# Cluster-routed attention with an ELU feed-forward on one core: query masks move to VectorE, the products lag one block more, and the weight conversion is spread more thinly

## The chip, the core and the metric

The kernel runs on one core of a Trainium2 chip. The core has a matrix engine (TensorE, PE in the profile, with its weight loads as PEld), three engines for elementwise work (VectorE is DVE, ScalarE is ACT, GpSimd is POOL) and a queue for transfers (SP). Each engine works through its own instructions in order and waits for the others through semaphores. The metric is the device time of one execution in microseconds (us).

## The reference, cut to what matters

```python
# q, k, v: (4 batches, 8 heads, 768 tokens, 64) float32; centroids: (8 heads, 16, 64)
q_assign = argmax(q_n @ c_n.T)            # nearest of 16 centroids for each query ...
k_assign = argmax(k_n @ c_n.T)            # ... and each key, by normalised rows
mask   = q_assign[:, :, :, None] == k_assign[:, :, None, :]
scores = where(mask, q @ k.T / 8, -1e9)   # a query sees the keys of its own cluster
attn   = softmax(scores)
x      = (attn @ v)  ->  (3072 tokens, 512)
h      = x @ w_in                         # w_in: (512, 2048)
g      = where(h > 0, h, exp(min(h, 0)) - 1)
out    = g @ w_out                        # w_out: (2048, 512)
```

The inputs q, k, v and the centroids are float32. The two weight matrices are float64 (float32 numbers divided by a numpy square root), so the kernel gets 64-bit words and makes float32 of them on the chip.

## The kernel before

**Blocks.** A batch has three thirds of 256 queries and four pairs of heads, so there are 48 blocks (batch, third, pair). The main loop runs over n: it finishes block n-1 (`values`), prepares the mask of block n+1 (`masks`), makes the scores of block n (`scores`), and then takes one group of the feed-forward, LAG blocks behind. A third of a batch has four groups: two calls of `hidden`, two more with a closing `finish`, four products of `outer`, three products of `outer`. (The seven products stand for eight by sums of blocks, a Strassen-like scheme, which is why the weights are summed once.)

In the code below the line numbers that the profile uses are put beside the lines as comments; `...` marks cuts.

```python
def masks(n):                                   # hot: one-hot cluster of each token, bf16
    b, third, pr = blocks[n]
    qm[n] = route.tile([P, QS], BF16, name="qm", tag="qm", bufs=2)
    for e in range(2):
        rows = slice(64 * e, 64 * e + 64)
        m = big[rows, pr % 2 : pr % 2 + 1]
        nc.gpsimd.tensor_scalar(                                        # L374
            qm[n][rows], hot[b, 0][rows, side(pr, e), ts(third, QS)],
            m, m, op0=Alu.mult, op1=Alu.subtract)

LAG = 6

def scores(n):
    ...
    for u in range(NT // 2):                    # three times a block
        s = banks()                             # one of three PSUM slots
        ...                                     # q.k on PE, L401
        ...                                     # + hot_k . qm on PE (the mask), L410
        nc.scalar.activation(p, s, Act.Exp, scale=SCALE)                # L418
        if n < LAG + 2:
            weigh(1)

def sums(n):                                    # three adds on VectorE   L424, L425, L426
    ...
def values(n):
    d = banks()[:, 0]
    summed = osum.pop(n, None)
    ...                # p.v into o_bank, 24 matmul instructions          # L447
    ...                # row sums of p: 24 instructions, or 4 where sums(n) has run   # L436
    nc.scalar.copy(x, o_bank[:, :QS])                                   # L461
    nc.scalar.activation(r, d[:, :QS], Act.Copy, accum_out=...)         # L463
    nc.vector.reciprocal(r, r)                                          # L464
    nc.gpsimd.tensor_tensor(x, x, r, op=Alu.mult)                       # L465

def hidden(b, third, n):
    h = banks()
    ...                                         # 32 matmul instructions, L486
    nc.scalar.activation(t, hf, Act.Exp)                                # L496
    nc.gpsimd.tensor_scalar(t, t, 1.0, 0.0, op0=Alu.min, op1=Alu.max)   # L497
    finish()                                    # the elu of the hidden before this
    lag.append(lambda: elu(n, t, hf))
def elu(n, t, hf):
    nc.vector.scalar_tensor_tensor(t, t, -1.0, hf, op0=Alu.add, op1=Alu.max)   # L503
    ...                                         # and a sum of blocks, L505 or L507
```

**Conversion of the weights.** `weigh(k)` takes the next k of 34 steps. The 32 pieces (16 of w_in, 16 of w_out, 128 x 512 each) pass through three consecutive steps each:

```python
for n in range(len(pieces) + 2):
    if n < len(pieces):
        e = exps[n] = loads.tile([P, WC], U32, name="ex", tag="ex", bufs=3)
        nc.vector.tensor_scalar(pieces[n][0], high, 0xFFFFF, ...)       # L244
        nc.vector.tensor_scalar(e, high, 0x7FF00000, ...)               # L247
    if 0 <= n - 1 < len(pieces):
        nc.scalar.activation(ex, ex, Act.Relu, scale=8.0, bias=off)     # L250
        nc.gpsimd.tensor_scalar(to, to, 2.0**-20, 1.0, ...)             # L251
    if n > 1:
        nc.vector.scalar_tensor_tensor(ex, w[:, :, 1], ..., ex, ...)    # L257
        nc.vector.scalar_tensor_tensor(to, w[:, :, 0], ..., to, ...)    # L260
        nc.gpsimd.tensor_tensor(to, to, ex, op=Alu.mult)                # L263
        ...
    yield
```

When all are done, `sum_weights` makes sums of blocks of w_out, in two halves: per half two GpSimd operations (L295, L296) and two VectorE ones (L297, L298).

**The main loop.**

```python
for n in range(len(blocks) + LAG):
    b, at = n // NB, n % NB                     # NB = 12 blocks a batch
    if 0 < n <= len(blocks): values(n - 1)
    ...
    if n + 1 < len(blocks) and at + 1 < NB: masks(n + 1)
    if n < len(blocks): scores(n)
    if 0 < n <= len(blocks): check(n - 1)       # L471
    if n < len(blocks):
        if n >= LAG + 2: sums(n)
        if ahead and at in turns: ...           # transposes of q and k of the next batch, L310
    beside = []
    if ahead and at + 1 == NB:                  # last block of a batch: clusters of the next
        beside = [None, similar(q), assign(q), similar(k), assign(k), masks(n + 1)]
    main = groups[n - LAG] if n >= LAG else []
    if n == LAG + 2:
        weigh(100)
        for half in range(2): sum_weights(half)
    for m, step in enumerate(main):
        step()
        ...                                     # beside is dealt out evenly behind the steps
        if n < LAG + 2: weigh(2)
```

`similar` is a matmul (L331) and a VectorE transpose (L338); `assign` is a chain on VectorE (L348, L350, L360, L363) that ends in `hot`.

Of the kernel before, what the change touches and what calls it, by code (L numbers as in the profile page):

```python
# [60 lines left out]
def main_path(ctx, tc, c, q, k, v, centroids, moe_w_in, moe_w_out, out):  # L61
    nc = tc.nc
# [31 lines left out]
    def banks():  # L94
        return short.tile([P, 2, 512], F32, name="banks", tag="banks")
# [13 lines left out]
    def load(name, i):  # L109
        b, pr = pairs[i]  # L110
        src = {"q": q, "k": k, "v": v}[name]
        if (name, i) in staged:
            t = first[:, ts(staged[name, i], 2 * NT * D)]
        elif name == "v":
            t = loads.tile([P, 2 * NT * D], F32, name="v_raw", tag="v", bufs=2)
        else:
            t = loads.tile([P, 2 * NT * D], F32, name=f"{name}_raw", tag="raw", bufs=4)
        if name == "v" or name == "q" and b == 0:
            t = t.rearrange("p (h t d) -> p h t d", h=2, t=NT)
            nc.sync.dma_start(  # L120
                t.rearrange("p h t d -> p h (t d)"),
                src[b, 2 * pr : 2 * pr + 2].rearrange("h (p t) d -> p h (t d)", t=NT),
            )
        elif b == 0:
            t = t.rearrange("p (t h d) -> p t h d", t=NT, h=2)
            for e in range(2):
                nc.sync.dma_start(
                    t[:, :, e], src[b, 2 * pr + e].rearrange("(p t) d -> p t d", t=NT)
                )
        else:  # L130

            for e in range(2):
                for g in range(2):
                    at = 64 * e + 32 * g
                    nc.sync.dma_start(
                        t[at : at + 32].rearrange("p (t a d) -> p t a d", t=NT, d=32),
                        src[b, 2 * pr + e, :, 32 * g : 32 * g + 32].rearrange(
                            "(a p t) d -> p t a d", a=4, t=NT
                        ),
                    )  # L140
        raw[name, i] = t
# [133 lines left out]
    def weigh(n):  # L275
        for _ in range(n):
            next(rest, None)
# [87 lines left out]
    def side(pr, e):  # L365
        return int(pr // 2 != e)

    def masks(n):
        b, third, pr = blocks[n]
        qm[n] = route.tile([P, QS], BF16, name="qm", tag="qm", bufs=2)  # L370
        for e in range(2):
            rows = slice(64 * e, 64 * e + 64)
            m = big[rows, pr % 2 : pr % 2 + 1]
            nc.gpsimd.tensor_scalar(  # L374
                qm[n][rows],
                hot[b, 0][rows, side(pr, e), ts(third, QS)],
                m,
                m,
                op0=Alu.mult,
                op1=Alu.subtract,  # L380
            )


    LAG = 6

# [3 lines left out]
    def scores(n):  # L391
        b, third, pr = blocks[n]
        i = b * NPR + pr
        cols = ts(third, QS)
        for u in range(NT // 2):
            s = banks()
            for m in range(2):
                kt = 2 * u + m
                for e in range(2):
                    rows = slice(64 * e, 64 * e + 64)  # L400
                    nc.tensor.matmul(  # L401
                        s[:, e, ts(m, QS)],
                        lhsT=T[i, 1][rows, ts(kt, P)],
                        rhs=T[i, 0][rows, cols],
                        start=True,
                        stop=False,
                    )
                for e in range(2):
                    rows = slice(64 * e, 64 * e + 64)
                    nc.tensor.matmul(  # L410
                        s[:, e, ts(m, QS)],
                        lhsT=hot[b, 1][rows, side(pr, e), ts(kt, P)],
                        rhs=qm[n][rows],
                        start=False,
                        stop=True,
                    )
            p = pu[n, u] = probs.tile([P, 2, 2 * QS], F32, name="p", tag="p")
            nc.scalar.activation(p, s, Act.Exp, scale=SCALE)  # L418
            if n < LAG + 2:
                weigh(1)  # L420

    def sums(n):
# [5 lines left out]
# [6 lines that stand above are left out]
        def row_sums(p, m, kt, last):  # L434
            for e in range(2):
                nc.tensor.matmul(  # L436
                    d[64 * e : 64 * e + 64, :QS],
                    lhsT=ones,
                    rhs=p[:, e, ts(m, QS)],
                    start=(kt == 0),  # L440
                    stop=(kt == last),
                )

        for kt in range(NT):
            p, m = pu[n, kt // 2], kt % 2
            for e in range(2):
                nc.tensor.matmul(  # L447
                    o_bank[64 * e : 64 * e + 64, :QS],
                    lhsT=raw["v", n][:, e, kt],
                    rhs=p[:, e, ts(m, QS)],  # L450
                    start=(kt == 0),
                    stop=(kt == NT - 1),
                )
            if summed is None:
                row_sums(p, m, kt, NT - 1)
        if summed is not None:
            row_sums(summed, 0, 0, 0)
        if pr == 0:
            xT[b, third] = xtp.tile([P, KC, QS], F32, name="xT", tag="xT")
        x = xT[b, third][:, pr]  # L460
        nc.scalar.copy(x, o_bank[:, :QS])  # L461
        r = work.tile([P, QS], F32, name="r", tag="r", bufs=1)
        nc.scalar.activation(r, d[:, :QS], Act.Copy, accum_out=d_sum[:, n : n + 1])  # L463
        nc.vector.reciprocal(r, r)  # L464
        nc.gpsimd.tensor_tensor(x, x, r, op=Alu.mult)  # L465
        rs[n] = r

    def check(n):

        r = rs.pop(n)  # L470
        nc.scalar.activation(r, r, Act.Copy, accum_out=r_sum[:, n : n + 1])  # L471
# [131 lines left out]
    def load_v(n):  # L603
        b, third, pr = blocks[n]
        if n not in seen:
            seen.add(n)
            load("v", b * NPR + pr)
            raw["v", n] = raw.pop(("v", b * NPR + pr))
# [3 lines left out]
    for j in range(2):  # L612
        for pr in range(NPR):
            turn(pr, j)
        for half in range(2):
            similar(0, j, half)
            assign(0, j, half)
        if j == 0:
            masks(0)

    for n in range(len(blocks) + LAG):
        b, at = n // NB, n % NB
        ahead = b + 1 < B
        if n <= len(blocks) and n > 0:
            values(n - 1)
        if ahead:
            for pr in {5: [0], 6: [1], 9: [2], 10: [3]}.get(at, []):
                load("q", (b + 1) * NPR + pr)
                load("k", (b + 1) * NPR + pr)
        if n + 1 < len(blocks):  # L630
            load_v(n + 1)
        if n + 1 < len(blocks) and at + 1 < NB:
            masks(n + 1)
        if n < len(blocks):
            scores(n)
        if 0 < n <= len(blocks):
            check(n - 1)
        if n < len(blocks):
            if n >= LAG + 2:
                sums(n)  # L640
            if ahead and at in turns:
                for j in range(2):
                    turn((b + 1) * NPR + turns[at], j)
        beside = []
        if ahead and at + 1 == NB:
            beside.append(None)
            for j in range(2):
                beside.append(lambda b=b, j=j: [similar(b + 1, j, half) for half in range(2)])
                beside.append(lambda b=b, j=j: [assign(b + 1, j, half) for half in range(2)])
            beside.append(lambda n=n: masks(n + 1))  # L650
# [3 lines that stand above are left out]
            for half in range(2):  # L654
                sum_weights(half)
        done = 0
        for m, step in enumerate(main):
            step()
            upto = len(beside) * (m + 1) // len(main)
            for other in beside[done:upto]:  # L660
                if other:
                    other()
            done = upto
            if n < LAG + 2:
                weigh(2)
        for other in beside[done:]:
            if other:
                other()
# [268 lines left out]
```

## Time and profile before

| | us |
|---|---|
| device time, median of three runs | 1076.47 (1075.84 to 1077.30) |
| span of the profiled execution | 1076.1 |
| VectorE busy in it | 523.3 (49%) |
| ScalarE busy | 292.8 (27%) |
| GpSimd busy | 332.2 (31%) |
| GpSimd in the query masks (L374), 96 instructions | 145.6, mean 1516 ns |

A row of the groups gives the line, the engine, the operation, what it writes and reads, how often, its busy time with the mean of one, and then the idle time of that engine just before it with what ended it. A busy PE is not PE at its peak, since the ends of matmuls are modelled. So the table of stretches (busy time of each engine between two moments) and the chain of waits say more of PE than its busy share.

### The profile page before, as it was taken

To read this page: it belongs to the slowest core of one execution; us is meant where nothing else is said; L and a number is where in the kernel's file an instruction comes from. 1 tells how busy PE (TensorE), PEld (TensorE's weight loads), DVE (VectorE), ACT (ScalarE), POOL (GpSimd) and SP (SyncE) were. 2 spreads that over 40 slices of the span, in tenths; PEclk is the share of its full clock that TensorE was granted. 3 is DMA by queue.
4 is the path that set the end of the run, shared out by engine and by line. 5 is a ranking of instruction groups with operands and counts; after the bars stand their busy time and mean duration, and the time that the engine had idled before them with its cause. 6 is when DMAs were issued, how large, how long until landed. Compare 5 with 4: busy or idle time off the path is not lost.

```text
span 1076.1 us, 14909 instructions
## 1 busy us (share of the span) xinstructions
PE 1014.5 (94%) x6363; PEld 785.1 (73%) x6363; DVE 523.3 (49%) x641; ACT 292.8 (27%) x499; POOL 332.2 (31%) x291
## 2 busy tenths in 40 slices
PE   7868785899999999999999999999999999999997
PEld 5545564676877877876887877876787877877885
DVE  5666677548425425538524425538534424424131
ACT  3544322132223123122223223122313223222010
POOL 2677778222322223122322222222322222221010
PEclk9999896999999999999999999999999999999999
DMA  9626511030001121230001120221000001000000
GB/s 286 243 69 162 137 55 30 15 79 16 16 35 42 34 64 30 44 69 27 15 35 38 37 64 30 44 65 30 16 35 30 16 35 31 16 35 1 20 1 23
DMA packets 103961, 55.60 MB, mean 52 GB/s; under 512 B 83408, under 2 KB 96720, under 8 KB 103888
## 3 DMA queue, kind: packets, MB, share of 16 engines
q1 hardware_dynamic: 103888, 54.57, 18.5%
q8 instruction: 52, 0.85, 0.3%
q14 instruction: 21, 0.17, 0.1%
HBM read 48.27 MB, written 6.29 MB: 51 GB/s over the span
## 4 chain that ended last, share of the span: by engine, by line
PE 78%; DVE 10%; POOL 8%; issue 3%; ACT 0%; DMA 0%; POOLq 0%; DVEq 0%
PE banks L486 27%; PE f_bank L516 15%; PE o_bank L516 11%; PE banks L401 10%; PE o_bank L447 10%; POOL qm L374 3%; PE banks L410 3%; DVE ex L257 2%; PE banks L436 2%; DVE r L464 1%; POOL w_in L263 1%; POOL w_out L263 1%; DVE ex L247 1%; DVE w_out L260 1%; DVE gT L503 1%
## 5 line engine op out<-in xcount | busy, mean ns | idle before, releaser
L486 PE MATMUL banks<-xT,w_in 128*128 128x256 f32 x1536 | 338.9, 381 | 0.3
L486 PEld LDWEIGHTS banks<-xT,w_in 128*128 128x128 f32 x1536 | 290.2, 190 | 48.2 <-issue 4.1
L401 PE MATMUL banks<-qT,kT 64*128 64x256 f32 x1152 | 175.8, 403 | 22.7 <-DVE gT L503 15.4
L418 ACT ACTIVATE p<-banks 128x1024 f32<-128x1024 f32 x144 | 147.2, 1022 | 52.3 <-PE banks L410 48.1
L447 PE MATMUL o_bank<-p,v_raw 128*64 128x256 f32 x1152 | 142.4, 384 | 11.1 <-ACT p L418 11.1
L374 POOL TENSOR_SCALAR qm<-hot,big 64x256 bf16<-64x256 bf16 x96 | 145.6, 1516 | 21.5 <-DVE hot L360 16.7
L464 DVE RECIPROCAL r<-r 128x256 f32<-128x256 f32 x48 | 84.0, 1750 | 133.7 <-ACT r L463 133.6
L401 PEld LDWEIGHTS banks<-qT,kT 64*128 64x128 f32 x1152 | 91.3, 194 | 75.0 <-DVE gT L503 16.7
L497 POOL TENSOR_SCALAR gT<-gT 128x1024 f32<-128x1024 f32 x48 | 51.2, 1067 | 277.3 <-ACT gT L496 277.3
L503 DVE SCALAR_TENSOR_TENSOR gT<-gT,banks 128x1024 f32<-128x1024 f32 x48 | 58.4, 1216 | 141.9 <-POOL gT L497 141.1
L447 PEld LDWEIGHTS o_bank<-p,v_raw 128*64 128x64 f32 x1152 | 78.1, 136 | 64.5 <-issue 16.1
L496 ACT ACTIVATE gT<-banks 128x1024 f32<-128x1024 f32 x48 | 49.1, 1022 | 275.5 <-PE banks L486 275.5
L465 POOL TENSOR_TENSOR xT<-xT,r 128x256 f32<-128x256 f32 x48 | 38.5, 801 | 274.6 <-DVE r L464 274.6
L516 PE MATMUL o_bank<-w_out,gT 128*128 128x256 f32 x384 | 91.4, 392 | 8.8 <-POOL w_out L296 8.7
L516 PEld LDWEIGHTS o_bank<-w_out,gT 128*128 128x128 f32 x384 | 73.7, 195 | 23.6 <-POOL w_out L296 9.9
L410 PE MATMUL banks<-qm,hot 64*128 64x256 bf16 x576 | 83.6, 276 | 4.5 <-DVE hot L360 4.4
L516 PE MATMUL f_bank<-w_out,gT 128*128 128x256 f32 x384 | 86.8, 379 | 0.0
L516 PEld LDWEIGHTS f_bank<-w_out,gT 128*128 128x128 f32 x384 | 73.0, 190 | 9.9
L461 ACT COPY xT<-o_bank 128x256 f32<-128x256 f32 x48 | 17.7, 369 | 219.6 <-PE o_bank L447 219.6
L424 DVE TENSOR_TENSOR psum<-p 128x1024 f32<-128x1024 f32 x40 | 51.7, 1293 | 37.8 <-ACT p L418 37.8
L425 DVE TENSOR_TENSOR psum<-psum,p 128x1024 f32<-128x1024 f32 x40 | 55.5, 1387 | 4.4 <-ACT p L418 0.6
L516 PE MATMUL f_bank<-w_sum,g_sum 128*128 128x256 f32 x192 | 44.6, 386 | 1.2 <-DVE part L563 1.2
(108 smaller groups left out, 832.7 us busy)
## 6 DMA issues: line engine op xcount, KB each, us to landing
v_raw<-in_v_dram SPq DMA_DIRECT2D x48, 384.0 KB, 3.2
w_sum<-in_moe_w_out_dram SPq DMA_DIRECT2D x12, 512.0 KB, 3.6
out_dram<-o_sb SPq DMA_DIRECT2D x24, 256.0 KB, 2.0
q_raw<-in_q_dram SPq DMA_DIRECT2D x48, 96.0 KB, 3.2
k_raw<-in_k_dram SPq DMA_DIRECT2D x48, 96.0 KB, 3.3
w_sum<-in_moe_w_in_dram SPq DMA_DIRECT2D x8, 512.0 KB, 7.5
w_out<-in_moe_w_in_dram SPq DMA_DIRECT2D x8, 512.0 KB, 10.4
w_out<-in_moe_w_out_dram SPq DMA_DIRECT2D x4, 512.0 KB, 4.1
```

Of the source, the lines that this page charges most:

```text
L374: nc.gpsimd.tensor_scalar(qm[n][rows], hot[b, 0][rows, side(pr, e), ts(third, QS)], m, m, op0=Alu.mult, op1=Alu.subtract,)
L401: nc.tensor.matmul(s[:, e, ts(m, QS)], lhsT=T[i, 1][rows, ts(kt, P)], rhs=T[i, 0][rows, cols], start=True, stop=False,)
L410: nc.tensor.matmul(s[:, e, ts(m, QS)], lhsT=hot[b, 1][rows, side(pr, e), ts(kt, P)], rhs=qm[n][rows], start=False, stop=True,)
L418: nc.scalar.activation(p, s, Act.Exp, scale=SCALE)
L424: nc.vector.tensor_tensor(to, pu[n, 0], pu[n, 1], op=Alu.add)
L425: nc.vector.tensor_tensor(to, to, pu[n, 2], op=Alu.add)
L447: nc.tensor.matmul(o_bank[64 * e : 64 * e + 64, :QS], lhsT=raw["v", n][:, e, kt], rhs=p[:, e, ts(m, QS)], start=(kt == 0), stop=(kt == NT ...
L464: nc.vector.reciprocal(r, r)
L486: nc.tensor.matmul(hf[:, f], lhsT=w_in[:, ch, ts(4 * n + f, P)], rhs=xT[b, third][:, ch], start=(ch == 0 and f % 2 == 0), stop=(ch == KC - 1),
L497: nc.gpsimd.tensor_scalar(t, t, 1.0, 0.0, op0=Alu.min, op1=Alu.max)
L503: nc.vector.scalar_tensor_tensor(t, t, -1.0, hf, op0=Alu.add, op1=Alu.max)
L516: nc.tensor.matmul(to[:, :QS], lhsT=left[:, f], rhs=right[:, f], start=(f == 0), stop=(f == FC // 2 - 1),)
```

## The change

The query masks go from GpSimd to VectorE. The feed-forward runs seven blocks behind attention instead of six. The conversion takes one step behind each score slot in ten blocks instead of eight, and one step instead of two behind each call of `hidden`; `sums` begins with block LAG (7) instead of LAG + 2 (8). It is meant to take work off GpSimd in the stage in which the weights are converted, and to have no place in that stage where several conversion steps come in a row.

```diff
@@ masks(n)
-            nc.gpsimd.tensor_scalar(
+            nc.vector.tensor_scalar(
                 qm[n][rows],
                 hot[b, 0][rows, side(pr, e), ts(third, QS)],
                 m,
...
-    LAG = 6
+    LAG = 7
@@ scores(n)
             nc.scalar.activation(p, s, Act.Exp, scale=SCALE)
-            if n < LAG + 2:
+            if n < LAG + 3:
                 weigh(1)
@@ main loop
         if n < len(blocks):
-            if n >= LAG + 2:
+            if n >= LAG:
                 sums(n)
...
             if n < LAG + 2:
-                weigh(2)
+                weigh(1)
```

By the code, the 34 steps were dealt out as three each in blocks 0 to 5, seven in block 6 and nine in block 7 (the rest, none, in block 8). Now it is three each in blocks 0 to 6, five in block 7, six in block 8 and two in block 9. The weight sums and the first products of `outer` come in block 9 instead of block 8.

## The prediction

> **What bounds the kernel now.** I read the page first, then the busy time by stretches cut at the reciprocals (one stands at the end of each block, so they mark the rounds of the loop), then the waits of the first 191 us, then one round in order of time, then the chain of waits.
>
> ```profile
> PE 1014.5 (94%) x6363; PEld 785.1 (73%) x6363; DVE 523.3 (49%) x641; ACT 292.8 (27%) x499; POOL 332.2 (31%) x291
> ...
> PE   7868785899999999999999999999999999999997
> ...
> PEclk9999896999999999999999999999999999999999
> ```
>
> After the seventh slice PE is at nine tenths to the end; before, it isn't. The stretches say the same in us:
>
> ```profile
> core 0: us, PE busy (x) PEld busy (x) DVE busy (x) ACT busy (x) POOL busy (x), PEclk, DMA share, GB/s
> 62.87:76.80 13.93, 9.50 (x84) 5.60 (x84) 8.96 (x14) 5.93 (x12) 10.65 (x9) 1.00 0.13 39
> 104.65:135.06 30.41, 23.17 (x134) 17.20 (x134) 21.93 (x33) 10.54 (x18) 21.58 (x19) 0.87 0.52 139
> 135.06:171.99 36.93, 27.17 (x159) 20.19 (x156) 29.55 (x41) 11.14 (x19) 25.83 (x22) 0.83 0.13 40
> 171.99:191.48 19.49, 10.75 (x41) 8.31 (x40) 14.89 (x11) 1.69 (x4) 18.62 (x8) 0.82 0.26 40
> 191.48:1076.10 884.62, 872.51 (x5334) 687.00 (x5334) 393.39 (x444) 223.43 (x384) 205.78 (x184) 1.00 0.13 33
> ```
>
> From 191.48 on PE is busy for 872.5 of 884.6 us at full clock: nothing on GpSimd matters there. So the change can pay only before 191.48, and it can cost something at the three places after it where a batch begins. A plain round of the early stage is 13.93 us long, with PE busy for 9.5; so something else sets its length. The waits from 34.91 to 191.48:
>
> ```profile
> ACT ex L250 <- DVE ex L247: 78.4, 28, 4.7
> DVE ex L247 <- POOL w_in L263: 24.8, 10, 3.8
> PE banks L401 <- DVE gT L503: 15.4, 3, 7.2
> PE o_bank L516 <- POOL w_out L296: 8.7, 2, 5.8
> ```
>
> The first two are the conversion waiting for itself, the third PE waiting for a PSUM slot that an elu on VectorE frees late, the fourth PE waiting for the sums of weights. One plain round in order of time (start, length, engine):
>
> ```profile
> 62.79 1.74 DVE L464 RECIPROCAL r<-r 128x256 f32<-128x256 f32 x1
> 62.95 1.27 POOL L263 TENSOR_TENSOR w_in<-w_in,ex 128x512 f32<-128x512 f32 x1 [1.23 <-DVE w_in L260]
> ...
> 64.61 0.78 POOL L465 TENSOR_TENSOR xT<-xT,r 128x256 f32<-128x256 f32 x1 [0.39 <-DVE r L464]
> 64.73 0.94 DVE L247 TENSOR_SCALAR ex<-w_out 128x512 uint32<-128x512 uint32 x1
> 65.38 3.74 POOL L374 TENSOR_SCALAR qm<-hot,big 64x256 bf16<-64x256 bf16 x2
> ...
> 69.21 0.62 POOL L251 TENSOR_SCALAR w_in<-w_in 128x512 f32<-128x512 uint32 x1
> 69.91 1.27 POOL L263 TENSOR_TENSOR w_in<-w_in,ex 128x512 f32<-128x512 f32 x1
> 71.22 0.43 DVE L247 TENSOR_SCALAR ex<-w_out 128x512 uint32<-128x512 uint32 x1 [3.80 <-POOL w_in L263]
> 71.56 1.10 DVE L257 SCALAR_TENSOR_TENSOR ex<-w_out,ex 128x512 uint32<-128x512 uint32 x1
> 72.58 0.68 DVE L260 SCALAR_TENSOR_TENSOR w_in<-w_out,w_in 128x512 f32<-128x512 uint32 x1
> 73.34 1.39 POOL L263 TENSOR_TENSOR w_in<-w_in,ex 128x512 f32<-128x512 f32 x1 [1.22 <-DVE w_in L260]
> ```
>
> The loop is L263, then L247 of the next step (which needs the exponent buffer that L263 frees, three in all), L257, L260, L263: 73.34 - 69.91 = 3.43 us a step. Three steps are some 10.4 us. The rest of 13.93 is that L263 at 69.91 comes late, because the two masks stand before it on GpSimd from 65.38 to 69.12.
>
> **What the Trainium skill says.** "SBUF — State Buffer", section "SBUF: two separate sides": VectorE and GpSimd share a pair of ports as an exclusive lock, taken for a whole instruction. The trace agrees: L247 takes 0.94 us beside L465 and 0.43 otherwise; a mask takes between 1.21 and 2.43 us. "VectorE: DVE Perf Modes", section "The perf-mode tier table (the rule you actually need)": a tensor_scalar with bf16 in SBUF has the same tier as a copy, four elements a cycle. The nearest row of this trace is the bf16 copy L363, 64x384 in 264 ns; a tensor_scalar with a scalar per partition (L189, 128x64) takes 250 ns. My estimate from these two rows is 0.28 us for a mask on VectorE, 0.55 us for a pair. "TensorE: Matmul & The Clock Gate", section "What's actually happening": PE's clock is halved after some 3.4 us of idling. Four L401 matmuls took 1.23 us at 127.68 behind 5.65 us of idling, 0.70 us otherwise, so the trace shows it, though not at quite a half.
>
> **The change part by part.**
>
> Start. The masks of blocks 0 and 1 now stand in VectorE's row, which was gapless from 18.7 to 27.4 us: 2 x 0.55 us more, less some 0.3 us of port contention with the masks that goes. The first reciprocal waits for ScalarE behind PE's values of block 0, and moves from 34.91 to about 35.2.
>
> Plain rounds, reciprocal to reciprocal. VectorE was busy for 8.96, plus 0.55 to 0.9 for the pair of masks (they can meet L465 at the lock), and idle for 1.2 us twice, before the second and third L247, while L263 runs; the 3.80 us wait behind the masks becomes one of these. 8.96 + 0.8 + 2.4 = 12.2 us for 13.93. PE's 9.5 and GpSimd's 10.65 - 3.74 = 6.9 lie within it. There are six such rounds, to the reciprocal of block 6: 35.2 + 73.2 = 108.4. (Before, five, to 104.65.)
>
> The two rounds with `hidden`, before 30.41 + 36.93 = 67.3 us with 16 steps. A step is 2.45 us of VectorE (L244 0.4, L247 0.4, L257 1.0, L260 0.65). Block 7 now: reciprocal 1.74, masks 0.6, five steps 12.25, `sums` 3.45 (1.3 + 1.4 + 0.75), one elu 1.95 (1.22 + 0.7), waits for L263 2.4, clamps at the lock 0.5: 23 us. PE has 14.0 for `hidden`, 3.4 for values, 3.9 for scores, together 21.3, so the round is nearly in balance. Block 8: 1.74 + 0.6 + six steps 14.7 + `sums` 3.45 + transposes 1.9 + three elus 5.85 + 2.4 + 0.5 = 31 us. Together 54: the reciprocal of block 8 is at 162.4, where that of block 7 was at 171.99.
>
> Weight sums. GpSimd needs about 12.5 us for its four operations (178.89 to 191.43). Before, they waited for L465 and the masks and began 7 us after the reciprocal. Now the last two L257 and L260 pairs come after the reciprocal and masks (0.6 + 2 x 1.7 + L263), so they begin after some 6.5: about 19 us for 19.49. The second half of the third product can run at 162.4 + 19 = 181.4.
>
> The rest. From the same point on there were 884.6 us. One attention block more lies behind: 6.6 us, read in the chain of waits from the values of a block to the next product, 198.61 to 205.24:
>
> ```profile
> 198.61 2.74 PE o_bank L447 x24
> 205.24 3.65 PE f_bank L516 x16
> ```
>
> A batch's last block now has two `hidden` calls beside the clusters of the next batch instead of three steps, and the masks follow both halves of assign(k) on VectorE. Before, PE waited at 265.05 only for the first half of the one-hot keys (0.66 and 0.27 us), and GpSimd had made the masks by then. Now one elu less stands ahead of assign(k), so it starts 2 us earlier behind similar(k), but PE needs its second half (2.4 us) and 0.55 us of masks: 1.2 us a batch, three times 3.6. One more `hidden` to product passage without attention between at the end: 0.3. So 884.6 - 6.6 + 3.9 = 881.9, and 181.4 + 881.9 = 1063.3. With the 0.4 us between span and median that is 1063.7, say 1063.5 us, 1.2% less.
>
> **The rivals.**
>
> *GpSimd was the whole bound*: with 3.74 us gone a round falls to 10.4 us (three steps of the loop). This gives 6 x 1.8 = 11 us more, about 1053. Against it: VectorE's own 9 us of work, to which the masks are added, and 2.4 us of waits in the loop don't fit in 10.4.
>
> *VectorE becomes the bound and the masks are dear there*: if a mask takes 0.5 us, or each pair waits for GpSimd's L465 to the end, rounds stay at 12.8 and blocks 7 and 8 grow by 3 (`sums` and transposes come in the same queue as the elus that free PE's slots): 6 x 0.6 + 3 + three batches at 1 = 10 us less gain, about 1073. For it speaks that VectorE was already busy for 29.55 of 36.93 in block 7's round.
>
> *It is hidden anyway*: PE could catch up what it idles. Against it: after 191.48 it has no slack to give back, so what the early stage gains stays gained.
>
> *Lag alone*: a block more before the products could only delay them, were PE not idle. Between 34.91 and 191.48 it is busy for 114.3 of 156.6 us (the sum of all eight stretches), so most of the 6.6 us moves into idle time.
>
> **Range and chances.** The uncertain terms are the round (12.2, plus or minus 0.5, six times: 3 us), blocks 7 and 8 (plus or minus 4) and the batches (plus or minus 3); in squares 5.8, so 8 in 10 within about 7: 1056 to 1070. A gain of 2% needs 1054.9, which takes the first rival nearly whole: 0.08. A loss of 2% needs a fault that no view shows: 0.01.
>
> **What would show it right or wrong.** Distances of reciprocals of 12.2 us in blocks 1 to 6; VectorE masks of 0.3 us; the wait of L247 for L263 at 1.2 us everywhere and never at 3.8; the reciprocal of block 8 near 162; the long stretch of gapless PE beginning near 181 rather than 191; at the three batch starts about 2 us of PE waiting for the masks rather than the one-hot keys. I'd be wrong in kind if the rounds kept their 13.9 us, or if PE waited after 190 us for VectorE in ordinary blocks.

## The result and the profile after

The changed kernel takes 1069.32 us (median; 1068.58 to 1070.75), the kernel before, measured beside it, 1076.72. The ratio is 0.9934, with a 95% interval of 0.9916 to 0.9951: 7.4 us or 0.66% faster. The profiled execution has a span of 1066.4 us. These two page rows answer to those of before (busy us and instructions, and the tenths of 40 slices):

```profile
PE 1011.3 (95%) x6343; PEld 784.4 (74%) x6343; DVE 559.3 (52%) x740; ACT 293.8 (28%) x499; POOL 188.9 (18%) x195
...
PE   6988876999999999999999999999999999999996
...
PEclk9999886999999999999999999999999999999999
```

GpSimd has lost 143 us of work and VectorE has gained 36, though the 96 masks alone are 45.2 there (470 ns each in the mean) and one block more has `sums`: other VectorE instructions became shorter, L247 from 19.3 to 14.2 us in sum. The stretches of the kernel after, the first four from reciprocal to reciprocal as before, then cut at the start of the second half of the third product (183.38) and of the fifth product (198.56):

```profile
core 0: us, PE busy (x) PEld busy (x) DVE busy (x) ACT busy (x) POOL busy (x), PEclk, DMA share, GB/s
57.73:69.79 12.06, 9.00 (x74) 5.51 (x72) 9.68 (x16) 5.44 (x12) 7.10 (x7) 0.86 0.15 46
105.99:130.22 24.23, 20.07 (x108) 15.51 (x108) 21.67 (x29) 8.13 (x15) 15.65 (x13) 0.88 0.29 100
130.22:161.74 31.52, 24.94 (x138) 18.56 (x136) 28.91 (x39) 11.04 (x18) 17.80 (x15) 0.82 0.29 71
161.74:183.38 21.64, 12.20 (x51) 8.85 (x46) 21.44 (x16) 2.55 (x5) 18.90 (x9) 0.74 0.23 36
183.38:198.56 15.18, 15.15 (x89) 10.66 (x89) 7.91 (x9) 3.27 (x6) 0.73 (x1) 0.81 0.08 27
198.56:1066.40 867.84, 853.02 (x5183) 674.80 (x5182) 401.56 (x504) 215.71 (x370) 91.01 (x106) 0.99 0.13 32
```

A plain round is 12.06 us long instead of 13.93, and VectorE is now the fullest engine in it. The two rounds with `hidden` are together 55.75 us, and the stretch with the weight sums has become longer (21.64 for 19.49). The waits of 34 to 190 us (total, times, longest) and one plain round in order of time:

```profile
ACT ex L250 <- DVE ex L247: 53.7, 25, 4.3
...
DVE ex L247 <- POOL w_in L263: 11.6, 10, 1.2
...
PE banks L401 <- DVE gT L503: 8.3, 3, 3.1
...
PE o_bank L516 <- POOL w_out L296: 8.1, 2, 5.3
```

```profile
69.95 1.27 POOL L263 TENSOR_TENSOR w_in<-w_in,ex 128x512 f32<-128x512 f32 x1 [1.23 <-DVE w_in L260]
71.45 0.96 DVE L374 TENSOR_SCALAR qm<-hot,big 64x256 bf16<-64x256 bf16 x2
71.61 0.73 POOL L465 TENSOR_TENSOR xT<-xT,r 128x256 f32<-128x256 f32 x1 [0.38 <-DVE r L464]
...
73.24 0.41 DVE L247 TENSOR_SCALAR ex<-w_out 128x512 uint32<-128x512 uint32 x1
...
74.93 1.38 POOL L263 TENSOR_TENSOR w_in<-w_in,ex 128x512 f32<-128x512 f32 x1 [1.89 <-DVE w_in L260]
```

No L247 waits 3.8 us any more: the longest is 1.2. The pair of masks takes 0.96 us: over all pairs the first mask takes 0.24 us in the median and the second, which meets L465, 0.72.

**Where the time is, in two parts.** I cut every trace at the start of the fifth product, the first moment at which no conversion work is left (198.56 us here, 205.24 before). With lag 7 one attention block more, 6.63 us, is done by then. So the early part gained 205.24 - 198.56 + 6.63 = 13.3 us, and the rest, 867.84 us for 870.86 - 6.63 = 864.23, lost 3.6. The difference, 9.7, is that of the spans; the medians give 7.4. The spans of the four runs of after differ by 2.3 us, so a single profiled execution is good to 1 or 2 us.

### The profile page after: what moved, and what is told of

Read it like the earlier page. It is cut to its first block, busy times and chain, and to the rows that moved or that the text cites. A ratio compares the mean times of both kernels' runs of the same rounds, so it can differ in the third digit from the quotient of the medians.

```text
span 1066.4 us, 14860 instructions
## 1 busy us (share of the span) xinstructions
PE 1011.3 (95%) x6343; PEld 784.4 (74%) x6343; DVE 559.3 (52%) x740; ACT 293.8 (28%) x499; POOL 188.9 (18%) x195
## 4 chain that ended last, share of the span: by engine, by line
PE 82%; DVE 13%; POOL 4%; issue 1%; DMA 0%; ACT 0%; DVEq 0%; POOLq 0%
PE banks L486 29%; PE f_bank L516 16%; PE o_bank L516 12%; PE banks L401 10%; PE o_bank L447 10%; PE banks L410 3%; DVE ex L257 2%; PE banks L436 2%; DVE r L464 1%; POOL w_in L263 1%; POOL w_out L263 1%; DVE ex L247 1%; DVE qm L374 1%; DVE w_in L260 1%; DVE w_out L260 1%; PE banks L331 1%
## 5 line engine op out<-in xcount | busy, mean ns | idle before, releaser
L401 PE MATMUL banks<-qT,kT 64*128 64x256 f32 x1152 | 174.5, 401 | 8.5 <-DVE gT L503 8.3
L503 DVE SCALAR_TENSOR_TENSOR gT<-gT,banks 128x1024 f32<-128x1024 f32 x48 | 58.4, 1216 | 156.8 <-POOL gT L497 156.7
L401 PEld LDWEIGHTS banks<-qT,kT 64*128 64x128 f32 x1152 | 91.7, 195 | 60.1 <-issue 11.3
L496 ACT ACTIVATE gT<-banks 128x1024 f32<-128x1024 f32 x48 | 49.1, 1024 | 280.9 <-PE banks L486 280.9
L497 POOL TENSOR_SCALAR gT<-gT 128x1024 f32<-128x1024 f32 x48 | 52.8, 1100 | 320.0 <-ACT gT L496 320.0
L465 POOL TENSOR_TENSOR xT<-xT,r 128x256 f32<-128x256 f32 x48 | 35.0, 729 | 318.7 <-DVE r L464 318.7
L410 PE MATMUL banks<-qm,hot 64*128 64x256 bf16 x576 | 82.9, 276 | 8.6 <-DVE qm L374 5.4
L424 DVE TENSOR_TENSOR psum<-p 128x1024 f32<-128x1024 f32 x41 | 50.2, 1224 | 13.0 <-ACT p L418 12.7
L425 DVE TENSOR_TENSOR psum<-psum,p 128x1024 f32<-128x1024 f32 x41 | 52.9, 1290 | 5.0 <-ACT p L418 1.6
L374 DVE TENSOR_SCALAR qm<-hot,big 64x256 bf16<-64x256 bf16 x96 | 45.2, 470 | 1.0
## 6 DMA issues: line engine op xcount, KB each, us to landing
w_out<-in_moe_w_in_dram SPq DMA_DIRECT2D x8, 512.0 KB, 10.4
```

Source lines behind the costliest of these rows:

```text
L374: nc.vector.tensor_scalar(qm[n][rows], hot[b, 0][rows, side(pr, e), ts(third, QS)], m, m, op0=Alu.mult, op1=Alu.subtract,)
L401: nc.tensor.matmul(s[:, e, ts(m, QS)], lhsT=T[i, 1][rows, ts(kt, P)], rhs=T[i, 0][rows, cols], start=True, stop=False,)
L410: nc.tensor.matmul(s[:, e, ts(m, QS)], lhsT=hot[b, 1][rows, side(pr, e), ts(kt, P)], rhs=qm[n][rows], start=False, stop=True,)
L424: nc.vector.tensor_tensor(to, pu[n, 0], pu[n, 1], op=Alu.add)
L425: nc.vector.tensor_tensor(to, to, pu[n, 2], op=Alu.add)
```

## The experiments

The theory on record is the prediction's: GpSimd's masks delayed the conversion, and their going shortens the early rounds; the batch starts pay a little of it back. The rivals are that lag and spread do the work, that VectorE's queue is where the gain is lost, or that the weight sums on GpSimd are. The medians of before beside each group of runs lie between 1076.7 and 1077.3 us.

### Which part of the change does it

`e1_masks_only` is the kernel before with only the engine of the masks changed:

```diff
-            nc.gpsimd.tensor_scalar(
+            nc.vector.tensor_scalar(
```

> The kernel before with one edit: the masks on VectorE (lag 6, 34 steps dealt out as before). My theory (VectorE's queue sets the early rounds, and masks at the end of VectorE's row hurt at a batch start): rounds of 12.1 us as in the changed kernel, five of them, 9 us gained; blocks 6 and 7 some 3 us, the weight sums 3 us; but with lag 6 a closing elu stands ahead of the second assign at a batch start, so the masks come 4.3 us after PE asks for them instead of 1.8: three times 3.3 us lost against the kernel before. Together about 1070 us. Rival A (GpSimd was the bound and the masks bring everything): 1069 too, but with batch starts as before. Rival B (the lag and the spreading bring everything): 1076.

`e2_masks_back` is the kernel after with only that line put back (lag, spread and `sums` stay).

> The changed kernel with the masks back on GpSimd (lag 7 and thin conversion stay). My theory: rounds of 13.9 us again, six of them (11 us lost), blocks 7 and 8 some 4 us longer, sums of weights begin 2 us later behind the masks, 2.7 us won back at the batch starts: about 1080 us, slower than both kernels. Rival B (lag and spreading bring the gain): 1069 as the changed kernel, or less.

Measured: 1078.16 us for the masks alone (ratio 1.0012, 1.0006 to 1.0019), 1075.04 for the rest alone (0.9983, 0.9975 to 0.9990). By itself the first costs 0.1% and the second gains 0.2%; the two don't add up to 0.66%. The cut at the fifth product says why:

| gain against before, us of span | early part | rest |
|---|---|---|
| masks alone (e1) | 205.24 - 190.20 = 15.0 | 870.86 - 884.6 = -13.7 |
| lag, spread and `sums` alone (e2) | 205.24 - 214.77 + 6.63 = -2.9 | 864.23 - 860.0 = 4.2 |
| both (after) | 13.3 | -3.6 |

The masks make all of the early gain: plain rounds take 12.06 us in e1 and 12.07 in after, 13.93 in e2 and before. With lag 6 they give it back later, and the same loss can be seen where a batch begins, here the first (start, length, engine; in brackets the idle time before and what ended it), in e1 and then in the kernel after:

```profile
244.05 1.50 PE L331 MATMUL banks<-kT,cT 128*32 128x384 f32 x16
...
253.25 0.65 PE L410 MATMUL banks<-qm,hot 64*128 64x256 bf16 x2 [3.90 <-DVE qm L374]
```

```profile
231.47 1.50 PE L331 MATMUL banks<-kT,cT 128*32 128x384 f32 x16
...
238.57 0.65 PE L410 MATMUL banks<-qm,hot 64*128 64x256 bf16 x2 [1.80 <-DVE qm L374]
```

From the clusters (L331) to the first mask product (L410) e1 takes 9.20 us, after 7.10, before 5.96 and e2 5.14. So the lag does help here: a batch now ends on a group without a closing elu, as the prediction read from the code. Both expectations missed here: e1 (1070 us) counted on 9.9 us of loss at the three starts and had 13.7 in the rest, and e2 (1080 us) on 2.7 won back there against after and had 7.8 in the rest (867.84 - 860.0).

### The batch start

The masks of a new batch need only `assign` of q, but they are issued behind `assign` of k, and on VectorE that is now the same queue. `e4_mask_early` is after with them one place earlier:

```diff
                 beside.append(lambda ...: [assign(b + 1, j, half) for half in range(2)])
-            beside.append(lambda n=n: masks(n + 1))
+                if j == 0:
+                    beside.append(lambda n=n: masks(n + 1))
```

> The changed kernel with the masks of a batch's first block put right behind the clusters of the queries, ahead of those of the keys, instead of behind both. My theory: PE's wait for the mask (1.8 us, three times) goes, and the first half of the one-hot keys is there in time: 2 us a batch, 6 us in all, 1063. Rival (PE then waits just as long for the one-hot keys): 1068 to 1069.

`e10_masks_split` takes the other way: only masks of blocks below 10 on VectorE, the later ones on GpSimd, which has little to do then.

> The changed kernel with the masks on VectorE only up to block 10 (while weights are converted and summed), and on GpSimd from there. My theory (masks on VectorE pay in the first 190 us and cost at the three batch starts, by standing behind both one-hot chains in one queue): batches 241.4 us apart as with the early mask, 9 to 10 us less than the changed kernel, 1059 us. Rival (the loss at the batch starts has another cause, such as PE's clock): 1066 or more.

Measured: e4 1058.96 us (0.9833, 0.9817 to 0.9849), 10.4 less than after; e10 1062.27 (0.9862, 0.9846 to 0.9879). The same moment in e4 has no wait:

```profile
231.72 1.50 PE L331 MATMUL banks<-kT,cT 128*32 128x384 f32 x16
236.32 0.70 PE L401 MATMUL banks<-qT,kT 64*128 64x256 f32 x4
236.85 0.28 PE L410 MATMUL banks<-qm,hot 64*128 64x256 bf16 x2
```

The three waits of after sum to only 5.4 us. A part of the other half is in the clock. The second batch start of after:

```profile
482.35 0.69 PE L410 MATMUL banks<-qm,hot 64*128 64x256 bf16 x2 [1.79 <-DVE qm L374]
...
483.69 0.43 PE L410 MATMUL banks<-qm,hot 64*128 64x256 bf16 x2
...
484.76 0.43 PE L410 MATMUL banks<-qm,hot 64*128 64x256 bf16 x2
```

Two such pairs start 1.07 us apart, where e4 has 0.54. So has the first batch start of after, behind its wait of 1.80 us:

```profile
239.49 0.28 PE L410 MATMUL banks<-qm,hot 64*128 64x256 bf16 x2
...
240.03 0.28 PE L410 MATMUL banks<-qm,hot 64*128 64x256 bf16 x2
```

The stretches around the batch starts, first of after (second, third start), then of e4 (first, second), show it in PEclk, the third figure from the end:

```profile
475.00:487.00 12.00, 10.09 (x80) 5.87 (x80) 9.01 (x20) 3.61 (x6) 1.77 (x2) 0.86 0.12 35
720.00:733.00 13.00, 11.09 (x85) 6.47 (x84) 10.21 (x21) 4.29 (x7) 1.77 (x2) 0.87 0.11 32
```

```profile
232.00:240.00 8.00, 7.97 (x80) 4.69 (x72) 7.27 (x16) 3.74 (x6) 1.04 (x1) 1.00 0.19 49
473.00:482.00 9.00, 8.97 (x84) 5.31 (x83) 8.24 (x20) 4.29 (x7) 1.14 (x2) 1.00 0.16 46
```

A share of 0.86 in 12 us is some 3.4 us at half clock (an estimate: 12 x 0.14 x 2). From one batch start to the next, after takes 243.78 and 245.20 us, e4 241.44; from the third to the end of the span they take 345.95 and 342.30. So 2.3 us are lost at the first start, 3.8 at the second and 3.7 at the third, together 9.8 of e4's 10.4. The first start lost its 2.3 us at full clock (1.8 of waiting, and the first matmuls behind it take longer: 0.65 us for L410 instead of 0.28), so the clock accounts for the 1.4 more at each of the other two, some 2.8 us.

e10 has the same gain there (241.44 twice), but the mask of block 10 now stands on GpSimd ahead of the last L263s and the weight sums: the first sum starts at 173.00 instead of 170.69. That takes the missing 3 us.

`e7_lag6` asks whether lag 7 is needed once the mask is early: e4 with `LAG = 6`.

> As the run with the early mask at the batch starts, but lag 6 instead of 7 (conversion then ends in block 8, with three steps more in it). My theory (an attention block of 6.6 us moves into idle time of PE): 4 to 7 us longer than the run with the early mask and lag 7, about 1068. Rival (lag 7 only delays the products by a round): 5 us shorter, about 1058.

Measured: 1077.14 us (0.9999, 0.9990 to 1.0007), 18.2 slower than e4 and 9 above what I expected. In spans, 17.7: of these 11.5 lie after the fifth product (876.2 - 6.63 = 869.6 for 858.1), and a batch takes 245.16 us again. With lag 6 the batch ends on a group of three steps, the last a closing `finish`. The six entries of `beside` are dealt out two to a step, so the mask call, now the fourth, moves `similar` of k behind that `finish`. On VectorE the transpose L338 (256.44 us) then stands behind the closing elu L503 (254.57), which waits 1.44 us for the clamp on GpSimd; in before L338 came first (260.01, L503 at 261.38). The masks themselves are long done (253.13), and PE waits for the keys:

```profile
259.19 0.57 PE L410 MATMUL banks<-qm,hot 64*128 64x256 bf16 x2 [1.41 <-DVE hot L360]
```

The other 6.2 are early; there PE waits for the last converted pieces of w_out, which the second product needs (total, times, longest):

```profile
PE f_bank L516 <- POOL w_out L263: 12.6, 4, 5.5
```

So the place of the mask call and the lag are not separate choices: the early call gains 10.4 us with lag 7 and next to nothing with lag 6 (1077.14 us against 1078.16 in e1, whose conversion is also spread differently).

### The rounds with `hidden`

`e3_sums_late` lets `sums` start two blocks behind the first `hidden` (block 9), as before the change:

```diff
-            if n >= LAG:
+            if n >= LAG + 2:
                 sums(n)
```

> The changed kernel with the row sums of blocks 7 and 8 left to PE, as LAG + 2 had it (the adds on VectorE, 4.7 us a block in the trace of the changed kernel, go; PE gets 2.3 us a block more). My theory (VectorE is the bound in blocks 7 and 8): the two rounds fall from 24.2 and 31.5 us to some 22.5 and 28, 4 us in all, 1065 us. Rival (PE is the bound there, as in the late stage): 4.6 us longer, 1074.

`e6_lumps` puts the old spread of the conversion into after (a step behind each score slot in nine blocks, two behind each call of `hidden`):

```diff
-            if n < LAG + 3:
+            if n < LAG + 2:
                 weigh(1)
...
             if n < LAG + 2:
-                weigh(1)
+                weigh(2)
```

> The changed kernel with the old dealing of conversion steps: two behind each call of hidden, none in block 9 (21 steps in blocks 0 to 6, seven in block 7, six in block 8). My theory (VectorE's work sets blocks 7 and 8, so where the steps stand moves only two of 34 steps ahead of the last reciprocal): 0 to 4 us longer, 1069 to 1073. Rival (lumps delay the elus that free PE's slots, and spreading is what brings the gain): 1075 or more.

Measured: e3 1062.17 us (0.9863, 0.9847 to 0.9880), 7.2 less than after; e6 1071.88 (0.9949, 0.9932 to 0.9965), 2.6 more. In e3 the rounds of blocks 7 and 8 take 154.71 - 106.42 = 48.3 us instead of 55.75. VectorE in after, in block 7:

```profile
118.11 1.21 DVE L424 TENSOR_TENSOR psum<-p 128x1024 f32<-128x1024 f32 x1
119.43 2.11 DVE L425 TENSOR_TENSOR psum<-psum,p 128x1024 f32<-128x1024 f32 x1
121.57 1.41 DVE L426 TENSOR_TENSOR psum<-psum 128x512 f32<-128x512 f32 x1
...
125.19 1.21 DVE L503 SCALAR_TENSOR_TENSOR gT<-gT,banks 128x1024 f32<-128x1024 f32 x1
```

The sums (4.7 us) stand in front of L503, the elu that frees a PSUM slot, and PE waits for that elu and then works at a lower clock (1.22 us for four L401 instead of 0.70):

```profile
126.46 1.22 PE L401 MATMUL banks<-qT,kT 64*128 64x256 f32 x4 [2.68 <-DVE gT L503]
```

In e3 the elu starts at 122.87 and this wait is gone:

```profile
124.61 0.70 PE L401 MATMUL banks<-qT,kT 64*128 64x256 f32 x4
```

The twenty row-sum matmuls that `sums` spares PE in each of these blocks cost less than that: in e3 they take five times 0.43 us a block, 4.3 us in all. PE's waits for elus and sums in the two rounds fall from 10.7 to 2.5 us, and the rest is clock: granted are 1.00 and 0.96 in e3's two rounds, 0.88 and 0.82 in after's. In e6 PE waits 13.6 us for elus instead of 8.3: the even spread is worth something, but less than half of what the early `sums` takes.

### The weight sums

`e5_wsums_dve` puts the first two sums on VectorE and moves the conversion's end and the sums ahead of `sums` and the transposes in that block:

```diff
-        nc.gpsimd.tensor_tensor(t1, f_, e_, op=Alu.subtract)
-        nc.gpsimd.tensor_tensor(f_, h_, f_, op=Alu.subtract)
+        nc.vector.tensor_tensor(t1, f_, e_, op=Alu.subtract)
+        nc.vector.tensor_tensor(f_, h_, f_, op=Alu.subtract)
```

> The changed kernel with all eight operations of the weight sums on VectorE (four were on GpSimd), ahead of the adds and transposes of block 9. My theory (PE waits 8.1 us for L296 on GpSimd, which takes 12.6 us for four operations under the shared ports; one such operation takes 1.2 us on VectorE alone): PE's waits for L296 fall to some 2 us, the fourth product starts 5 to 7 us earlier, 1063 us. Rival (VectorE is as much the bound there, and the adds, transposes and evictions behind the sums come late): no more than 2 us, 1067 to 1070.

Measured: 1068.44 us (0.9929, 0.9908 to 0.9951), which is no clear difference from after. The sums on GpSimd (after) and on VectorE (e5):

```profile
170.69 3.32 POOL L295 TENSOR_TENSOR w_sum<-w_out 128x1024 f32<-128x1024 f32 x1
```

```profile
169.84 1.21 DVE L295 TENSOR_TENSOR w_sum<-w_out 128x1024 f32<-128x1024 f32 x1
```

They became nearly three times as fast, and the waits show that PE got little of it, since a new wait came:

```profile
PE f_bank L516 <- DVE o_sb L553: 5.2, 1, 5.2
...
PE o_bank L516 <- DVE w_out L296: 3.3, 2, 2.8
```

L553 takes the second product out of PSUM. It now stands behind all of `sums` and the transposes, and began at 186.47. `e8_all` puts e3, e4 and e5 together; `e9_reordered` also takes the sums that the third product needs first and puts `sums` and the transposes of block 9 behind the second product:

```diff
+            for part in range(2):             # L295, L296 of both halves, then L297, L298
+                for half in range(2):
+                    sum_weights(half, part)
...
             step()
+            if n == LAG + 2 and m == 1:
+                later()                       # sums(n) and the transposes
```

> The changed kernel with the three edits together: early masks at batch starts, weight sums on VectorE, row sums of blocks 7 and 8 on PE. My theory: the gains are at different places and add up, 4 + 6 + 6 us: about 1053. Rival (they share one queue, so each takes what another gave): 1060.

> The version with the three edits together, and one more: in block 9 VectorE does the four sums that PE waits for first, then the other four, then the evictions, and the adds and transposes of that block only behind the second product. My theory (the weight sums on VectorE brought nothing alone because the eviction of the second product stood behind 5 us of adds and transposes; PE waited 5.2 and 5.5 us for it): the wait goes, the fourth product starts near 175 us instead of 179.9, and less idling spares PE some slow clock: 1047 us. Rival (the sums themselves are what the fourth product waits for): 1051 to 1052.

Measured: e8 1052.23 us (0.9763, 0.9747 to 0.9779), e9 1046.92 (0.9722, 0.9706 to 0.9739). The gains of e3 and e4 against after (7.15 + 10.36 = 17.5) add up to e8's 17.1, so they are separate faults; the weight sums on VectorE (0.9 alone) bring nothing visible here either. In e9 the fifth product starts at 185.9 us, 12.7 before that of after, and the spans differ by 22.4. PE still waits once, for the eviction of the second product (L555 is L553 here), since the last sums (L299 and L300 in this version, 1.22 us each, four of them) stand ahead of it in VectorE's queue:

```profile
174.06 5.24 PE L518 MATMUL f_bank<-w_sum,gT 128*128 128x256 f32 x16 [4.27 <-DVE o_sb L555]
```

So the expectation had the time right, not the cause: the wait did not go, it fell from 5.48 us in e8 to 4.27. Counted from the first reciprocal (35.41 us in e8, 34.47 in e9), the fourth product starts 4.9 us earlier; 2.4 of these are there when the second half of the third product starts (171.09 and 167.80), where the new order of the sums counts, 1.3 come from that half running faster (1.99 us for 3.30) and 1.2 from the shorter wait. The two edits of e9 were not run apart.

e9 is the best version that I ran: 2.8% faster than before and 2.1% (22.4 us by the medians) faster than after. That remaining wait I didn't try to remove.

## Why the prediction was right, and where its sum was off

The direction held, and the time lies in the range, at its upper edge (1063.5 in 1056 to 1070; 1069.3); of a gain of 13 us foreseen there were 7.4. By its steps, in spans (1063.3 foreseen, 1066.4 measured):

- **Start**: 35.2 foreseen, 33.56 measured. The start also moves between 33.6 and 35.4 in the other runs of the same beginning, so this is no finding.
- **Plain rounds**: 12.2 foreseen, 12.07 measured (105.99 - 33.56 over six), by the sum given: VectorE busy for 9.68 and two waits of 1.16 us. The first rival (10.4 us; its three steps of 3.43 are 10.3) is false. The mask, estimated at 0.28 us from a bf16 copy and a small tensor_scalar, took 344 ns in the median and 470 in the mean, up to 793 beside L465; a pair took 0.94 us in the mean, a little over the allowance (0.55 to 0.9).
- **Blocks 7 and 8**: 54 foreseen, 55.75 measured. The mis-sized term is `sums`: 3.45 foreseen, 4.7 in each of the two blocks. The Trainium skill has the lock of VectorE and GpSimd ("SBUF — State Buffer", "SBUF: two separate sides"), and I charged it to the clamps and masks, not to these adds: L425 takes 2.11 us here, and 1.23 in e5's block 9, where GpSimd is quiet. The reciprocal of block 8 still came at 161.74 (162.4 foreseen), since the start and the plain rounds were early.
- **Weight sums**: 19 foreseen, 21.64 measured, the largest error before the cut. The four operations took 12.65 us, as foreseen (12.5). They began 8.95 us after the reciprocal instead of 6.5. The terms listed for that, with the reciprocal itself, come to 7.0; the rest is that masks, L260 and L263 took longer beside each other (1.03 us for 0.6, the last L260 1.75 for 0.68, the last L263 2.18 for 1.27):

```profile
166.28 1.65 POOL L263 TENSOR_TENSOR w_out<-w_out,ex 128x512 f32<-128x512 f32 x1 [1.22 <-DVE w_out L260]
168.55 2.18 POOL L263 TENSOR_TENSOR w_out<-w_out,ex 128x512 f32<-128x512 f32 x1 [0.62 <-DVE w_out L260]
```

- **Not foreseen**: behind the weight sums PE runs at a lower clock (0.81 in 183.38 to 198.56, where before had 0.88 in the same passage), and the same 89 matmuls took 15.18 us instead of 13.76: 1.4 us.
- **The rest**: 3.6 us of loss at the batch starts foreseen and 3.6 measured. The way from the clusters to the first mask product grew by 1.14 us (7.10 for 5.96), where 1.2 was worked out. The sum is right, the parts are not: a batch takes 0.5 us longer at the first start (243.78 for 243.28), where before had waited twice, and 1.9 at the second (245.20 for 243.33), since the half clock at the later ones was not in it. That the sum fits is luck.
- **Offset**: I took 0.4 us between span and median. That figure was too small: it compared the median with a profiled execution of before that was itself above the median. In the runs of both kernels the time is 1.7 to 2.2 us above the span of the same run; of after, the profiled run was also 0.7 us below the median. So of the 5.8 us between 1063.5 and 1069.3, 3.1 are the span (1066.4 for 1063.3) and most of the rest is this term.

"It is hidden anyway" is false (the early gain stays). "Lag alone" is too kind: without the masks' move, lag, spread and `sums` together gained nothing early (-2.9 us) and paid only at the batch starts (+4.2). "VectorE becomes the bound" is half true, and its half that the prediction underrated is the order of VectorE's queue: 7.2 us go to the early `sums`, 10.4 to the place of one mask call, together more than twice the gain that is left. Both places could be read from the order of the instructions.

What stays open: which of lag, spread and `sums` makes the early 2.9 us of loss in e2 (e3 suggests `sums`, but with the masks on VectorE), so what the lag alone is worth early is not shown.

## What to carry to other kernels

When work is moved to another engine, its duration is the smaller question; ask behind what it now stands in that engine's queue and what stands behind it, above all the instructions that free a PSUM slot or end a wait of the busiest engine. Where such an engine has no slack, move the call, not only the engine: here one call issued earlier was worth more than the whole change. And speeding up an operation that others wait for may bring nothing (e5) until the order of that queue follows the order in which the others need its results (e9).

## What the hardware showed that I had not expected

**A short wait and the clock.** A wait of 1.8 us is enough to cost the clock, and whether it does depends on where it falls. The Trainium skill ("TensorE: Matmul & The Clock Gate", "What's actually happening") has the halving after an idle window of some 3.4 us and says that the window is free-running. The measured waits are shorter than that window, but the traces have its grid: the granted clock in them is full or half, and within a trace it changes only at distances that are multiples of 3.41 us. The batch start of after, with its wait of 1.79 or 1.80 us, stands twelve times in the traces of after, e3, e5 and e6:

| the wait | times | clock in the step of 3.41 us behind it |
|---|---|---|
| lies within one step (second and third start of after) | 8 | half, all 8 times |
| is cut by a border, at most 1.63 us in either step (first start of after: 0.30 and 1.50) | 4 | full, all 4 times |

So such a wait cost 2.3 us at full clock and up to 3.8 with the half clock, and which of the two changes from start to start. The length of the wait alone gives no rule: in e7 the half clock followed two of three waits of 1.41 us.

**The mask on two engines.** The mask, 64 x 256 bf16 with two scalars per partition, takes at least 1.21 us on GpSimd (e2, median 1.41) and at least 0.235 us on VectorE, while GpSimd does L497, 128 x 1024 float32 with immediate limits, in 1.10 us in the mean. The skill ("GPSIMD Engine Reference", "4.1 Engine selection") has operations with two inputs about twice as slow there as on VectorE and those with one input at "roughly line-rate". This form, with one tensor and two scalars read, was five times slower by the shortest and four times by the medians (1.41 and 0.344 us). Whether bf16 or the scalars per partition make it so, no run here shows.
